# A planner's schedule replaced by a written-out sequence, with the first filter load split in two

## The chip, the cores and the metric

The kernel runs on one core of one Trainium2 chip. Five engines take part, each with its own instruction queue that runs strictly in order: PE (TensorE, matmuls from SBUF into PSUM), DVE (VectorE), ACT (ScalarE), POOL (GpSimd) and SP (SyncE, which here only issues DMAs). They meet through semaphores. The metric is the device time of one execution in microseconds; the time before is the median of three runs.

## The reference

Two layers, each a long convolution mixer followed by an MLP, on a sequence of 2048 rows and 512 channels in bfloat16:

```python
x = A_q
x = x + _A_ref(_layernorm(x), A_k, A_v, A_shift_k, A_ssm_k, A_ssm_D)
x = x + _B_ref(_layernorm(x), B_w1, B_b1, B_w2, B_b2)
x = x + _A_ref(_layernorm(x), A_k, A_v, A_shift_k, A_ssm_k, A_ssm_D)
x = x + _B_ref(_layernorm(x), B_w1, B_b1, B_w2, B_b2)
```

`_A_ref(q, k, v, ...)` shifts `k` along the sequence with four taps per channel, multiplies it with `v` to give `kv`, convolves `kv` causally over 2048 steps with a filter `ssm_k` per channel (by FFT in the reference), adds `kv * ssm_D` and multiplies by `q`. `_B_ref` is a layernorm, a 512 to 1376 matmul with bias, GELU, and a 1376 to 512 matmul with bias. The convolution doesn't depend on `x`, so both layers use the same result `y`, and it is computed once.

## The kernel before

The convolution is an FFT written as small matmuls. A group is usually 16 matmuls that fill two of the eight PSUM banks (1024 float32 columns), and one instruction of ACT or DVE that evicts it to SBUF as bfloat16. The steps, with their PE and eviction lines:

- **ht**: the filters, loaded as four blocks of 128 channels (L679), are turned by 16 PE transposes each (L749) and evicted; `ssm_D` is added to one row (L755, "D" below).
- **h1** (16 groups, L766) and **h2** (16 groups, L779): the two stages of the filter's transform. Stage 2 multiplies by the 4 MB table `S`, which is loaded in 16 pieces.
- **swaps**: 16 DMAs inside SBUF (L647) that make a copy of the transformed filter with neighbouring partitions exchanged. The first eight need the first eight h2 groups, the others the rest.
- **fir**: the shift and `kv`. Channel blocks 0 and 1 go over PE: a turn of `k` (L810, evicted; "T") and two groups of diagonal matmuls (L827), each multiplied with `v` out of PSUM by DVE (L834; "m0", "m1"). Blocks 2 and 3 are eight DVE tensor-tensor instructions each (helper line L658).
- **x1** (16 groups, L766) and **x2** (two halves of eight groups, L872): the same two stages for `kv`. Each x2 group is evicted and then multiplied with the filter by DVE (L658, 128x2048; "P0" to "P7", and "P'0" to "P'7" for the second half).
- **i1** (two halves of eight groups, L896; the second is written `i1'`) and **i2** (ten groups, L953): the inverse stages, which leave `y` in SBUF. A half's i1 needs all eight products of that half.

All evictions of this part go through one helper (L663 on ACT, L664 on DVE). Then come the MLP layers. Layer 0 goes through the rows in blocks of 1, 1, 2, 2, 2, 2, 2, 2, 2 (times 128 rows), layer 1 in four blocks of 4. For each block: **q** (DVE statistics L985 and L987, a power on POOL L991 and L993, the normalization L1000), **y** (two DVE tensor-tensors per row tile), **z** (statistics and normalization again), a transpose (by PE for the first two row tiles, L1047; by a DMA for all others, L1039), **m1** (44 matmuls L1060, 11 GELUs on ACT L1065), **m2** (11 matmuls per row tile, L1093; the last tile in pieces, L1082) and the residual add on DVE (L1097). Row tiles are 16 per layer.

The order of all this isn't the order of the source. Every operation is recorded with estimated durations, reads and writes. A list planner (`schedule`) then places them, by a priority built from the longest path behind an operation, a bias per step (`BIAS`), a bias per operation (`PB`), times before which an operation is held (`HOLD`) and fixed engines for some evictions (`ENG`). DMAs get a priority that keeps them in the order of the source. The planner also gives out PSUM banks, within limits per pool:

```python
dconv = Pool(2, 4, True)
ptr, pm1, pm2 = Pool(1, 2), Pool(1, 3), Pool(1, 3)
```

`sync` then finds the semaphore waits that the resulting order needs, and `emit` writes the five queues.

Of the kernel before, what the change touches and what calls it, by code (L numbers as in the profile page):

```python
# [7 lines left out]
ALU = mybir.AluOpType  # L8
# [14 lines left out]
class Pool:  # L23


    def __init__(self, nb, cap, gate=False):
        self.nb, self.cap, self.used, self.gate = nb, cap, 0, gate


class Tile:  # L30


    def __init__(self, pool):
        self.pool = pool
        self.base = None
        self.left = 0
        self.ops = []


class Op:  # L40
    __slots__ = ("i", "engs", "eng", "fn", "dur", "preds", "succ", "prio", "tile", "dma", "start", "end",
                 "pos", "inc", "waits", "val", "npred", "ready", "bytes", "base", "extra", "gate", "tag", "allow")


class Prog:
# [5 lines left out]
    LAT = 155.0  # L51
    BIAS = {'': 1044190, 'fir0': 816272, 'fir1': 594035, 'fir2': 1000293455, 'fir3': 475782, 'h1': 868926, 'h2': 42492, 'ht': 880650, 'i1_0': 1240071, 'i1_64':
        1212024, 'i2_0': 1097582, 'i2_64': 1190749, 'm1': 1032413, 'm2': -1808312, 'q0': 602778, 'q1': 1095651, 'q19': 267875, 'q2': 1096365, 'q20':
        912832, 'q21': 583017, 'q22': 318772, 'q3': 998981448, 'q4': 986060, 'q5': 466064, 'q6': 470208, 'q7': 409268, 'q8': 641212, 'taps': 736508,
        'warm0': 1000949769, 'x1_0': 1331587, 'x1_1': 783401, 'x1_2': 1063685, 'x1_3': 949292, 'x2_0': 377017, 'x2_64': 955361, 'y0': 1650539, 'y1':
        1623078, 'y19': 2204116, 'y2': 1000018107, 'y20': 947043, 'y21': 1812233, 'y22': 1073869, 'y3': 1411221, 'y4': 607830, 'y5': 295728, 'y6':
        405240, 'y7': 620020, 'y8': 1895488, 'z0': 999281074, 'z1': 1641796, 'z19': 1050878, 'z2': 131483, 'z20': -312548, 'z21': 457235, 'z22':
        577125, 'z3': -403715, 'z4': 81537, 'z5': 198870, 'z6': -330710, 'z7': 181103, 'z8': 1650154}
    SHY = {'fir0': 1021, 'fir1': 277, 'h1': 55, 'h2': 0, 'ht': 0, 'i1_0': 0, 'i1_64': 365, 'i2_0': 61, 'i2_64': 0, 'x1_0': 0, 'x1_1': 8, 'x1_2': 1351, 'x1_3':
        1268, 'x2_0': 0, 'x2_64': 462, 'z0': 261, 'z1': 833}  # L60
    PB = {0: 150814, 1: -52106, 2: -225577, 3: -123331, 4: 999221868, 9: 1276405, 44: 1379512, 45: 1434690, 47: 506509, 49: 453148, 51: 999588645, 52:
        1000042154, 53: 1589169, 54: 1589469, 55: 1517533, 56: 1595021, 57: 1561543, 58: 1589849, 59: 1505754, 60: 1589135, 61: 1539763, 63:
        999477473, 64: 999472326, 65: 81483, 66: 1000044663, 67: 999459987, 68: 19356, 69: 999454615, 70: 999472376, 71: -54290, 72: 999450473, 73:
        999474703, 75: 999467239, 76: -144374, 77: 999428971, 78: 239791, 79: 999491599, 80: 245756, 81: 999824582, 82: 168731, 83: 999955057, 84:
        -153184, 85: 1000209098, 86: 182551, 87: 999183272, 88: 316431, 89: 999956485, 90: -132325, 91: 999955107, 92: 228777, 93: 999458556, 94:
        -263977, 95: 1000286130, 96: -155038, 97: 999951289, 98: 491335, 99: 999392283, 100: 370445, 101: 999956535, 102: 370055, 103: 999943327, 104:
        316481, 105: 1000160828, 106: 1184366, 107: 1000314641, 108: 1291204, 109: 1000854551, 110: 1266991, 111: 1000849866, 112: 1230810, 113:
        1262509, 114: 1184316, 115: 745385, 116: 899745, 117: 1262559, 118: 909647, 119: 1001022447, 120: 893995, 121: 1000704463, 122: 834188, 123:
        874451, 124: 883372, 125: 1000706919, 126: 774582, 127: 998790820, 128: 785190, 129: 1000706969, 130: 861289, 131: 998997835, 132: 820442,
        133: 998980303, 134: 656521, 135: 998997885, 136: 907870, 137: 998958853, 155: -39187, 156: -120533, 157: -28284, 158: -97856, 159: 55705,  # L70
        161: -516310, 162: -336038, 163: -518892, 164: 205143, 165: 997729962, 166: -214054, 167: -532152, 169: 999878049, 170: 26055, 171: 341414,
        172: 302525, 173: -46374, 175: -516143, 176: -99172, 177: 431557, 178: -1035368, 179: 998060916, 180: -4231, 181: 998061019, 183: -127374,
        184: -999854529, 185: -1000132297, 186: -999488136, 187: -999485498, 188: -999373078, 189: -999483119, 191: 998075025, 192: -336655, 193:
# [119 lines left out]
    def __init__(self, nc):  # L193
        self.nc = nc
        self.ops = []
        self.state = {}
        self.nodes = [(-1, None)]
        self.cache = {}
        self.tag = ""
# [62 lines left out]
    def op(self, eng, fn, dur, reads=(), writes=(), tile=None, dma=None, prio=0.0, nbytes=0, gate=()):  # L262
        o = Op()
# [10 lines left out]
        for t in o.tile:  # L274
            for p in t.ops:
                preds.add((p.i, "psum"))
            t.ops.append(o)
            t.left += 1
# [294 lines left out]
NWARM = 0  # L573
# [560 lines left out]
```

## Time and profile before

| what | value |
|---|---|
| time, median of 3 runs | 241.92 us (241.72 to 242.06) |
| the profiled execution: span from first to last instruction | 239.8 us |
| the profiled execution: other times | none is given |
| PE busy | 226.5 us (94%) |
| DVE busy | 175.7 us (73%) |
| ACT busy | 142.9 us (60%) |
| POOL busy | 34.8 us (15%) |
| granted TensorE clock | 1.00 throughout |
| moved by DMA | 27.40 MB, 385 GB/s in slices 2 to 4 of 40 |

The profile is of one execution. Busy shares are means over a span that has two very different parts: the convolution, up to about 84 us, in which PSUM groups are evicted one by one, and the MLP layers, in which PE streams long matmuls. A share over the whole span therefore says little; the chain of waits, the timelines and the windows are read by stage. Where a helper records many operations they share its line (L658, L663, L664), and the shape tells them apart.

### The profile page before, as it was taken

The numbers are of one execution on the slowest core, as the hardware profiler recorded it, in microseconds if no ns is written. First come the engines' busy times: TensorE is split into PE (matmuls) and PEld (weight loads), VectorE is DVE, ScalarE is ACT, GpSimd is POOL, SyncE is SP. The second block draws the span as 40 slices with busy tenths as digits, with TensorE's granted clock in tenths as the row PEclk, the third lists the DMA queues.
The fourth block names the chain that finished last, engine by engine and source line by source line (L and its number), as shares of the span: only waits on it lengthen the run. The fifth ranks groups of instructions, "written<-read, shape, count | busy, mean of one in ns | idle before, by whom it ended". The sixth has DMA issues, their size and how long they took to land.

```text
span 239.8 us, 5559 instructions
## 1 busy us (share of the span) xinstructions
PE 226.5 (94%) x2310; PEld 151.5 (63%) x2330; DVE 175.7 (73%) x363; ACT 142.9 (60%) x223; POOL 34.8 (15%) x75
## 2 busy tenths in 40 slices
PE   7988899886899999999999999999999999999996
PEld 3876777775899885777767665754444444444453
DVE  0779999999997989989999996978997401211214
ACT  3697999999998994665556253464532552436200
POOL 3250000000012222223141032022130100000000
PEclk9999999999999999999999999999999999999999
DMA  6999999999910004222020203313022203210022
GB/s 231 338 387 385 384 235 272 249 282 337 375 63 0 3 0 48 45 44 48 0 44 5 42 1 68 66 23 68 0 44 44 87 3 69 62 44 0 3 98 77
DMA packets 37035, 27.40 MB, mean 114 GB/s; under 512 B 19506, under 2 KB 29969, under 8 KB 37010
## 3 DMA queue, kind: packets, MB, share of 16 engines
q1 hardware_dynamic: 36446, 26.91, 38.1%
q8 instruction: 18, 0.29, 0.5%
q10 hardware_dynamic: 564, 0.14, 0.4%
q14 instruction: 7, 0.06, 0.1%
HBM read 16.82 MB, written 2.10 MB: 79 GB/s over the span
## 4 chain that ended last, share of the span: by engine, by line
PE 71%; DVE 15%; DMA 4%; ACT 4%; SPq 3%; issue 2%; DVEq 0%
PE ps L1060 32%; PE ps L1093 30%; DVE ar L658 8%; PE ps L896 5%; DMA ar<-in_A_v_dram 4%; ACT ar L663 4%; DVE ar L664 4%; SPq L647 3%; DVE ar L834 2%; PE ps L1082 1%; PE ps L872 1%; DVE sm L985 1%; PE ps L953 1%; DVE ar L1000 0%; PE ps L766 0%
## 5 line engine op out<-in xcount | busy, mean ns | idle before, releaser
L1065 ACT ACTIVATE ar<-ps,sm 128x256 bf16<-128x256 f32 (+5 forms) x143 | 67.8, 522 | 72.8 <-PE ps L1060 70.1
L1060 PE MATMUL ps<-ar 128*128 128x256 bf16 (+5 forms) x568 | 83.7, 296 | 0.2
L1093 PE MATMUL ps<-ar 128*128 128x512 bf16 (+1 forms) x329 | 78.9, 379 | 0.7
L663 ACT ACTIVATE ar<-ps 128x1024 bf16<-128x1024 f32 (+2 forms) x79 | 73.9, 1055 | 8.0 <-PE ps L766 3.2
L1060 PEld LDWEIGHTS ps<-ar 128*128 128x128 bf16 (+1 forms) x572 | 53.2, 100 | 29.4 <-ACT ar L1065 0.4
L658 DVE TENSOR_TENSOR ar<-ar 128x512 bf16<-128x512 bf16 (+3 forms) x108 | 63.8, 628 | 1.8 <-DMA ar<-in_A_k_dram 1.4
L1093 PEld LDWEIGHTS ps<-ar 128*128 128x128 bf16 (+1 forms) x341 | 33.2, 98 | 34.5
L1097 DVE TENSOR_TENSOR ar<-ar,ps 128x512 bf16<-128x512 bf16 x31 | 20.8, 682 | 43.2 <-PE ps L1093 43.1
L985 DVE BATCH_NORM_STATS2 sm<-ar 128x6 f32<-128x512 bf16 (+1 forms) x68 | 42.6, 650 | 0.3
L1000 DVE TENSOR_SCALAR ar<-ar,sm 128x512 bf16<-128x512 bf16 x64 | 24.1, 401 | 6.6 <-POOL sm L993 6.3
L993 POOL TENSOR_TENSOR sm<-sm 128x2 f32<-128x2 f32 (+2 forms) x26 | 20.5, 787 | 2.2
L766 PE MATMUL ps<-ar 128*64 128x128 bf16 x512 | 17.6, 221 | 3.0 <-DVE ar L664 1.0
L991 POOL TENSOR_SCALAR sm<-sm 128x2 f32<-128x2 f32 (+2 forms) x26 | 5.9, 226 | 95.9 <-DVE sm L987 95.7
L766 PEld LDWEIGHTS ps<-ar 128*64 128x64 bf16 x512 | 14.9, 110 | 5.4 <-DVE ar L664 1.3
L664 DVE CAST ar<-ps 128x1024 bf16<-128x1024 f32 (+1 forms) x15 | 17.5, 1181 | 0.4 <-PE ps L872 0.2
L896 PE MATMUL ps<-ar 128*128 128x128 bf16 x256 | 15.1, 220 | 1.0 <-DVE ar L658 0.5
L896 PEld LDWEIGHTS ps<-ar 128*128 128x128 bf16 x256 | 14.5, 114 | 1.4 <-ACT ar L663 0.8
L872 PE MATMUL ps<-ar 128*128 128x64 bf16 x256 | 9.6, 193 | 2.3 <-ACT ar L663 2.1
L664 DVE COPY ar<-ps 128x2048 bf16<-128x2048 bf16 (+1 forms) x6 | 5.7, 954 | 7.6 <-PE ps L749 7.4
L987 DVE BATCH_NORM_AGGREGATE sm<-sm 128x2 f32<-128x6 f32 (+1 forms) x64 | 10.8, 177 | 0.6
L872 PEld LDWEIGHTS ps<-ar 128*128 128x128 bf16 x256 | 8.2, 98 | 3.5 <-ACT ar L663 3.4
L779 PE MATMUL ps<-ar 128*128 128x128 bf16 x128 | 8.7, 220 | 0.9 <-ACT ar L663 0.8
(33 smaller groups left out, 72.0 us busy)
## 6 DMA issues: line engine op xcount, KB each, us to landing
ar<-tab_s SPq DMA_DIRECT2D x16, 256.0 KB, 10.0
ar<-ar SPq DMA_DIRECT2D x16, 256.0 KB, 4.6
ar<-in_A_ssm_k_dram SPq DMA_DIRECT2D x4, 512.0 KB, 5.5
ar<-in_A_k_dram SPq DMA_DIRECT2D x8, 256.0 KB, 7.7
ar<-in_A_v_dram SPq DMA_DIRECT2D x8, 256.0 KB, 9.7
ar<-in_A_q_dram SPq DMA_DIRECT2D x4, 512.0 KB, 7.8
out_dram<-ar SPq DMA_DIRECT2D x7, 256.0 KB, 2.0
ar<-in_B_w_dram SPq DMA_DIRECT2D x1, 1376.0 KB, 12.0
```

The lines of the kernel that those rows point to most:

```text
L658: return P.op(eng, lambda e: e.tensor_tensor(o, a, b, op), dur, reads=[a, b] + list(more), writes=[o])
L663: return e.activation(dst, src(), AF.Copy)
L664: return e.tensor_copy(dst, src())
L766: r = e.matmul(Q(tl, 64 * ri, 64, i * 128, [1, 128]), w, m, start=True, stop=True)
L896: r = e.matmul(Q(tl, 0, 128, i * 128, [1, 128]), w, m, start=q == 0, stop=q == 1)
L985: P.op(DVE, lambda e, sj=sj, x=x: e.bn_stats(sj, x), 40.0 + 1.1 * w, reads=[x], writes=[sj], gate=gate)
L993: P.op(POOL, lambda e: e.tensor_tensor(r, v, hf, ALU.pow), 430.0 + 150.0 * n, reads=[v, hf], writes=[r])
L1000: P.op(DVE, lambda e: e.tensor_scalar(o, x, m, r, ALU.subtract, ALU.mult), 335.0, reads=[x, m, r], writes=[o])
L1060: r = e.matmul(Q(tl, 0, rows, 0, [1, w]), a, m, start=dk == 0, stop=dk == 3)
L1065: P.op(ACT, lambda e, dst=dst, tl=tl, rows=rows, bias=bias, w=w: e.activation(dst, Q(tl, 0, rows, 0, [1, w]), AF.Gelu_apprx_tanh, bias=bia ...
L1093: r = e.matmul(Q(tl, 0, 128, 0, [1, 512]), ins[fc][0], ins[fc][1], start=fc == 0, stop=fc == 10)
L1097: P.op(DVE, lambda e, x=x, tl=tl: e.tensor_tensor(x, x, Q(tl, 0, 128, 0, [1, 512]), ALU.add), 640.0, reads=[x], writes=[x], tile=tl)
```

## The change

The planner and its tables are removed. In their place stands a list `ORDER` with the number of every operation, in one sequence over all engines; each engine's queue is that sequence, filtered. `SECOND` names the 20 operations that take the second of their possible engines, and `BANKS` the first PSUM bank of every tile. The limits per pool, the gates on some statistics and the estimated durations go. `sync` and `emit` stay as they were, but for how an eviction's engine is chosen.

One piece of the computation is cut differently: the filters are loaded, turned and evicted as five blocks, two of 64 channels and three of 128. That makes one DMA, one group, one eviction and one add more (1118 operations for 1114).

```diff
+HBLOCKS = ((0, 64), (64, 64), (128, 128), (256, 128), (384, 128))
...
-    for b in range(4):
-        dma(A(0, 128, R_HRAW + b * 2048, [1, 2048]), dr(A_ssm_k, b * 128 * 2048, [2048, 128], [1, 2048]), 1 << 19)
+    for c, n in HBLOCKS:
+        dma(A(c % 128, n, R_HRAW + c // 128 * 2048, [1, 2048]), dr(A_ssm_k, c * 2048, [2048, n], [1, 2048]))
...
+    for c, n in HBLOCKS:
+        tl = Tile(-(-n // 64))
+        src = [A(c % 128, n, R_HRAW + c // 128 * 2048 + a, [16, 128]) for a in range(16)]
+        idn = A(c % 128, n, R_ID + c % 128, [1, n])
...
+                r = e.transpose(QB(tl, 0, 128, a * n, [1, n]), src[a], idn)
...
+    ORDER = (
+        48, 49, 6, 0, 1, 66, 67, 9, 50, 51, 7, 75, 5, 3, 8, 69, 76, 2, 63, 13, 77, 52, 20, 4, 53, 70, 108, 109, 19, 12, 15, 104, 28, 14, 68,
...
+    SECOND = (
+        64, 67, 70, 71, 73, 74, 76, 81, 87, 93, 107, 171, 173, 183, 211, 217, 222, 291, 297, 328)
...
+    def arrange(self):
+
+        self.order = {e: [] for e in (PE, ACT, DVE, POOL, SP)}
+        last = [None] * 8
+        second = set(self.SECOND)
+        assert sorted(self.ORDER) == list(range(len(self.ops)))
+        for at, i in enumerate(self.ORDER):
+            o = self.ops[i]
+            o.eng = o.engs[i in second]
+            o.at, o.pos = at, len(self.order[o.eng])
+            self.order[o.eng].append(o)
+            tl = o.tile
+            if tl is not None and tl.base is None:
+                tl.base = self.BANKS[tl.i]
```

What the lists make of the queues, from the start to the last product (DVE and ACT) and to the first transposing DMA (SP). "ht0a" and "ht0b" are the half blocks (ht0 is block 0 before), "x1.c.n" is group n of channel block c, "fir2.0" to "fir2.7" are the instructions of a DVE channel, "q1" is a statistics instruction of block 1; on SP "k" are the filter blocks, K, V, S, T, X the pieces of `k`, `v`, the tables and `q`, "sw" the swaps.

```text
DVE before: ht0 D0 ht2 h1.2 D2 D1 ht3 D3 h1.6 h1.12 fir2.0 fir2.1 fir0.T fir3.0 fir2.2 fir3.1 fir0.m0
  fir3.2 fir2.3 fir3.3 fir0.m1 h2.3 fir2.4 h2.5 x1.0.0 fir2.5 fir3.4 fir2.6 fir1.m1 h2.8 fir2.7 fir3.5
  fir1.m0 fir3.6 x1.1.0 fir3.7 x1.2.3 x1.3.2 x2.3 P3 P1 P2 P0 P5 P7 P4 P6 P'3 P'0 P'2 P'7 P'1 P'4 P'6 P'5
DVE after: ht0b ht3 D3 ht1 D0b ht0a D0a h1.14 ht2 h1.7 h1.1 h1.4 fir3.0 fir2.0 fir2.1 fir1.T fir2.2
  fir3.1 fir1.m1 fir2.3 fir3.2 fir2.4 fir0.m1 fir2.5 fir2.6 fir3.3 fir0.m0 fir3.4 fir2.7 fir3.5 fir1.m0
  fir3.6 x1.0.3 fir3.7 x1.1.2 x1.3.0 x2.1 P2 P1 P3 P0 P6 x1.3.3 P7 P5 P4 P'3 q1 P'2 q1 P'1 P'0 P'7 P'6 P'5 P'4
ACT before: table tap tap ht1, 13 h1, fir1.T, 6 h2, 3 x1, 7 h2, 8 x1, x2.1 x2.2 x2.0 x2.5 x1.3.0
  x2.7 x2.4 x2.6 x2'3 x2'1 x2'0 x2'2 x2'7 i1.0 x2'4 i1.7 x2'6 x2'5
ACT after: table tap table tap, 12 h1, fir0.T, 14 h2, 2 x1, 2 h2, 6 x1, x2.2 x2.3 x2.0 x1.3.1 x1.2.1
  x2.6 x1.3.2 x2.7 x1.2.2 x2.5 x2.4 x2'3 x2'1 x2'2 x2'0 x2'7 i1.2 x2'6 x2'5 x2'4
SP before: k0 k1 k2 k3 2 halo, K0 to K7, V0 to V7, S0 to S15, tables, T3 sw0 to sw7, sw8 to sw15,
  T0 T1 T2 X0 X1 X2 X3 W1 W2
SP after: k0b k3 k1 k0a k2 K0 K7 K6 halo K2 V7 K1 K3 K5 K4 halo S0 V5 S3 S6 S13 S7 V6 S4 V4 S5 S12 S2
  V3 S10 S1 S15 S14 U S9 V2 V1 S11 V0 S8 bias sw1 sw0 sw5 sw2 bias sw3 sw11 sw14 sw10 sw6 sw15 sw9
  sw4 sw8 X2 T0 sw7 X1 T3 X0 bias T2 sw13 sw12 W2 W1 T1 X3
```

On POOL the adds D1 and D2 and two fills of borders now stand among the eight tap multiplies (L741 before). Behind the products, statistics of blocks 3, 4 and 5 stand earlier on DVE than before, block 0 comes before block 1 on PE (before it was the other way round), and PE's order of m1 and m2 groups is another, with the same groups in it.

## The prediction

> **What bounds the kernel now.** I read the chain that ended last first, in order of time, then each engine's timeline over the first 90 us, then the work in the stretch behind it. The chain:
>
> ```profile
> 52.62 2.29 ACT ar L663 x3
> 54.91 0.44 issue
> 55.35 0.87 ACT ar L663
> ...
> 64.70 3.84 PE ps L896 x64
> 68.63 8.21 PE ps L896 x144
> 76.83 0.45 PE ps L953 x4
> ```
>
> Columns are start, length, what. Up to 64.7 us the chain hops between VectorE and ScalarE, with PE pieces of half a microsecond between; from 64.70 it stays on PE (the 0.9 us pieces of VectorE at 78 to 83 us belong to block 0 and run while PE does the rest of `i2`). The window behind it:
>
> ```profile
> 84.70:237.50 152.80, 151.92 (x928) 88.26 (x941) 101.52 (x267) 68.66 (x144) 22.37 (x42) 1.00 0.18 39
> ```
>
> PE is busy 151.92 of 152.80 us at full granted clock: the two MLP layers have no hole to win. So the end is the moment at which PE becomes continuous, plus a fixed sum of matmuls. That moment is set by VectorE and ScalarE, which turn PSUM groups over. VectorE, then ScalarE:
>
> ```profile
> 16.80 2.36 DVE L658 TENSOR_TENSOR ar<-ar 128x2048 bf16<-128x2048 bf16 x2 [1.43 <-DMA ar<-in_A_k_dram]
> ...
> 50.23 18.25 DVE L658 TENSOR_TENSOR ar<-ar 128x2048 bf16<-128x2048 bf16 x16
> ```
>
> ```profile
> 18.53 1.94 ACT L663 ACTIVATE ar<-ps 128x1024 bf16<-128x1024 f32 x2 [0.53 <-PE ps L766]
> 21.03 1.94 ACT L663 ACTIVATE ar<-ps 128x1024 bf16<-128x1024 f32 x2 [0.56 <-PE ps L766]
> 23.57 2.88 ACT L663 ACTIVATE ar<-ps 128x1024 bf16<-128x1024 f32 x2 [0.60 <-PE ps L766]
> 26.75 14.78 ACT L663 ACTIVATE ar<-ps 128x1024 bf16<-128x1024 f32 x16 [0.31 <-PE ps L779]
> ```
>
> VectorE waits for `k` until 16.80 and then hardly stops until the last product ends at 50.23 + 18.25 = 68.48; PE starts the second half's `i1` 0.15 later, at 68.63. One 1024-column eviction steps at 14.78/16 = 0.92 us on ScalarE, one large VectorE instruction at 18.25/16 = 1.14.
>
> **Part 1, who evicts.** Between first tap and last product VectorE does 45 large instructions before: 16 of the two VectorE channels, 4 PSUM multiplies, 16 products, 9 evictions (fir0.T, three h2, four x1, one x2). That is 51.68/45 = 1.148 each with its small waits. After, 6 evictions are left (fir1.T, four x1, one x2), 42 instructions, and the statistics and their aggregate for `q1` stand between products: 0.60 + 0.10. The first tap still needs all of `k`, now with one 256 KB piece of `v` ahead in SP's queue: 0.262 MB at the 385 GB/s of slice 3 is 0.68, so 16.80 becomes about 17.5. Then 17.5 + 42 x 1.148 + 0.7 = **66.4** for the last product: 2.1 earlier, if nobody starves VectorE.
>
> ScalarE takes what VectorE gave. Up to the last product's eviction it does 55 evictions and one turn (1.88) before, and 56 and one turn after: 53.4 us. Before it begins at 9.48 and has to be done by 68.48 - 1.14 = 67.34; 9.48 + 55 x 0.92 + 1.88 = 62.0, so between 4 and 5 us of gaps lie in it (the rows above, and 0.70, 0.61, 0.44 and smaller ones). After it begins at about 9.2 (part 2): 62.6 plus gaps. Those at 18 to 24 us come from PE sitting behind `fir0.T` and a bank that VectorE held; after, that turn stands at the end of h1, and h2 finds its tables earlier (part 3). I count half the old gaps, 2.2: 64.8, the last product at about 66.0 by ScalarE against 66.4 by VectorE. The two rarely fit without loss; I take **67.0**, a gain of 1.5. The ends are 66.4 (no loss) and 68.3 (all old gaps, 62.6 + 4.5 + 1.2).
>
> **Part 2, the halves.** Before, the first turn starts at 4.97 (16 matmuls, 1.22 us) and four blocks need 4.9 us of PE. After, two half blocks with a 64-column operand (the 64-column matmuls of L872 go 16 in 0.64) and three whole ones: the same PE time. One eviction, one add and one DMA issue are new: about 0.65 for a half eviction (half of the 1.22 row; bounds 0 and 1.22), 0.22 for an add, 0.42 on SP. The half lands first and block 3 second, so a first h1 group can be evicted near 9.2 instead of 9.48, and ScalarE no longer has the 1.88 us turn of block 1. The turns lie before VectorE's wait for `k`, which covers 1.43 us; VectorE's list there (five turns, four h1, three adds) ends near 16.7, before `k`. If it ended later, each microsecond would go straight onto 17.5. A second table load (1.28, its row) now stands between the two tap evictions; ScalarE idles 1.28 there before, so nothing is late.
>
> Two of the adds and two small fills move onto POOL among the tap multiplies, whose eight take 5.55 us from 10.42 and end at 15.97 before. After, the last two or three run past 17 us, beside VectorE's tensor-tensors. No row of before shows that pair. Bounds: nothing, or 2 x 0.69 if VectorE waits out two; I take nothing and keep 1.4 for the range. The Trainium skill (SBUF — State Buffer, "SBUF: two separate sides") says that a GpSimd instruction reading SBUF and a VectorE one with two SBUF inputs exclude each other for a whole instruction; by it the same 1.4 us would be lost, and VectorE would finish at 67.8.
>
> **Part 3, the transfers.** SP's list is another: `S` tables and `v` pieces alternate, the upper swaps are mixed with `X` and `T` loads. Every swap is still behind the h2 evictions that it reads. By ScalarE's order the tenth h2 eviction (lower swaps may go) ends near 9.2 + 11.5 + 1.9 + 10 x 0.92 = 31.8, the sixteenth, with two x1 between, near 39.2; before, the swaps were issued at 32.79 and 41.56. Eight issues at 0.8 put the swap that product 6 needs at 45.6, plus the 4.6 us of the issue table: 50.2; VectorE gets there at 17.5 + 29 x 1.148 = 50.8. The `v` pieces for the first PSUM multiply are 7.0 MB into the queue; `k` landed at 16.80 when 5.2 MB had moved for 4.4 queued, so add 0.8: 7.8 MB have moved at about 23.4, needed at 24.4. These fit with half a microsecond; they are why I don't count 66.4.
>
> `q1` statistics between products wait for `X0`. Ahead of and with it the queue has 16.6 MB; the slices of before reach that sum at 54 us, plus 2 to land is 56. VectorE is there at 17.5 + 35 x 1.148 = 57.7. A later landing delays every product behind it.
>
> **Part 4, behind the products.** PE order puts one `i1` group more behind the last product matmul (14 for 13, 0.93 each), which is only moved. From the second half's first `i1` group the remaining PE work is 168.4 before and 167.5 after (nine and eight `i1` groups at 0.93, 64 `i2` matmuls at 0.113, m1 at 0.054 per matmul and 128 columns, m2 at 0.2165 per matmul); measured 237.49 - 68.63 = 168.86, so 0.4 is lost before. With that group at 68.2 (0.15 behind VectorE it could be 67.2; six groups of 0.93 behind the last product matmul near 62.6 make 68.2) PE would end at 68.2 + 167.9 = 236.1 against 237.49: 1.4 earlier.
>
> The lifted limits on MLP banks cost nothing either way: PE lost 0.4 there in all. The new order spends its slack here. From the last product to the norms of block 3, VectorE has 26.7 us of work after and 23.7 before (by 0.60, 0.34, 0.32 and 1.13 per row); from that first `i1` group PE has 30.3 to block 3's m1 after and 33.0 before. Slack is 3.6 + 1.2 against 9.3 + 0.15. The transposing DMA takes 2.5 to land, and VectorE idled 2.9 us from 68.5 to 95 before (its waits for POOL and PE). 4.8 - 2.6 - 2.9 = -0.7. The early statistics should remove part of the POOL waits; I charge 0.2.
>
> **Sum.** 1.4 - 0.2 = 1.2 earlier: span 239.8 - 1.2 = 238.6. The page gives no other time of its execution than the span; the median lies 241.92 - 239.8 = 2.1 above it, and I keep that: **240.7**.
>
> **Rivals.** (a) *The lists mesh fully*: last product at 66.4, first `i1'` group at 67.5, nothing lost behind: PE ends 237.49 - 2.1, time 239.8. For it: ScalarE's gaps had causes that the order removes. Against: fits of half a microsecond in part 3. Chance 0.22. (b) *The change doesn't do what it says*: ScalarE has 0.9 us more to do and keeps its 4.5 us of gaps, the last product stays at 68.3; about 241.8. Chance 0.14. (c) *The other side*: PE starves at block 3's m1 (or block 2's), because VectorE comes late with the norms. It decides when VectorE idles more than 2.2 us between 67 and 94; the kernel is slower than before from 2.2 + 1.4 = 3.6. With 5 us of idle (before's 2.9 and a 2 us wait for X loads) PE waits 2.8: 241.9 - 1.4 + 2.8 = 243.3. For it: a negative remainder in part 4. Against: before PE lost 0.4 in all there, and earlier statistics fill VectorE's waits. Chance 0.20. Forecast, 240.1 to 241.4: chance 0.44.
>
> **The numbers.** 0.2% of the time is 0.5 us, about what a measurement of this kernel tells from no change. Faster takes forecast and (a), 0.66; same (b), 0.14; slower (c), 0.20. The range runs from 239.3 (a with another half microsecond) into the lower part of (c), 242.7; two in ten are left out, most of them above. The forecast's own range is 240.1 to 241.4.
>
> **What would show it.** First tap at 17.2 to 17.8; last product ending at 66.4 to 67.5; ScalarE's gaps from 9 to 50 us under 3; first `i1` group of the second half at 67.3 to 68.5; PE busy over 99% behind it, PE's last matmul near 236.3. Wrong if VectorE's products wait for a DMA, if tensor-tensors beside POOL take over 1.3 us, or if m1 of the first four blocks waits for VectorE or the transposing DMA.

## The result, and the profile after

The changed kernel takes **245.62 us** (244.99 to 246.06, four runs) against 241.95 (241.72 to 242.06, four runs) for the one before on the same chip. The ratio is 1.0151, with a 95% interval of 1.0135 to 1.0167: slower by 3.7 us, where 1.2 faster was forecast. The profiled execution spans 244.3 us (before 239.8); it is the slowest of the four (246.06), so the difference of the spans, 4.5, is larger than that of the medians.

The chain that ended last, in order of time (start, length, what), at the two places that matter:

```profile
65.89 1.20 ACT ar L454
67.09 0.05 issue
67.14 9.31 PE ps L676 x160
...
91.38 0.78 PE ps L862 x4
92.16 3.98 DMA ar<-ar
96.14 0.04 issue
96.18 1.82 PE ps L829 x17
```

PE becomes continuous at 67.14 (before 64.70). And behind it there is a new hole: block 2's m1 waits for a transposing DMA that takes 3.98 us to land. Before, the same DMA takes 3.86 (issued at 90.37, landed at 94.23), and PE has m2 matmuls to do until then:

```profile
91.21 3.19 PE L1093 MATMUL ps<-ar 128*128 128x512 bf16 x14
```

From the issue on, PE had 3.90 of other work before; in the new order of m1 and m2 groups it has 2.52 (92.16 to 94.68). The late landing and the shorter cover make the wait together. The windows show that nothing else is lost there (PE busy is the second number after the window's length):

```profile
67.14:87.20 20.06, 20.06 (x292) 18.85 (x293) 19.70 (x48) 19.68 (x24) 4.62 (x12) 1.00 0.32 115
87.20:97.00 9.80, 8.30 (x111) 6.72 (x110) 9.70 (x31) 7.36 (x22) 4.53 (x9) 1.00 0.15 28
97.00:242.00 145.00, 144.99 (x844) 81.97 (x841) 88.31 (x231) 59.86 (x125) 19.62 (x34) 1.00 0.17 39
```

So the end comes 4.5 later: 2.44 from the moment at which PE becomes continuous, 1.50 from that wait, and 0.93 from the one i1 group that was moved behind the last product, less 0.4 of small losses that before has (all from the two profiled executions). The lists of VectorE and ScalarE show the first part. VectorE:

```profile
21.13 3.67 DVE L451 TENSOR_TENSOR ar<-ar 128x2048 bf16<-128x2048 bf16 x3
26.33 1.23 DVE L454 COPY ar<-ps 128x2048 bf16<-128x2048 bf16 x1 [1.54 <-PE ps L591]
...
65.52 6.87 DVE L451 TENSOR_TENSOR ar<-ar 128x2048 bf16<-128x2048 bf16 x6
```

Its first tap starts at 21.13 (before 16.80, forecast 17.5) and waits for no DMA: VectorE comes late from its h1 evictions. `k` itself is late too. Its last piece landed at 18.38 (before 16.78) and the halo, which the second tap needs, at 19.13, so that an early VectorE would have met 18.4 and not 17.5. It waits 1.54 for fir1.T's turn, and the last product ends at 72.39 (before 68.48). ScalarE:

```profile
13.40 2.85 ACT L454 ACTIVATE ar<-ps 128x1024 bf16<-128x1024 f32 x3 [4.18 <-PE ps L547]
16.65 7.44 ACT L454 ACTIVATE ar<-ps 128x1024 bf16<-128x1024 f32 x8 [0.40 <-PE ps L547]
25.33 57.64 ACT L454 ACTIVATE ar<-ps 128x1024 bf16<-128x1024 f32 x62 [1.24 <-PE ps L547]
```

The first h1 eviction starts at 13.40 (forecast 9.2). Before:

```profile
9.48 1.94 ACT L663 ACTIVATE ar<-ps 128x1024 bf16<-128x1024 f32 x2 [0.16 <-PE ps L766]
```

Behind its start, ScalarE idles only 0.40 and 1.24, less than was allowed for. TensorE says why it starts so late:

```profile
1.31 2.74 PE L500 MATMUL ps<-ar 128*128 128x512 bf16 x6 [1.31 <-POOL ar L494]
4.55 1.17 PE L530 MATMUL ps<-ar 64*128 64x64 bf16 x16 [0.50 <-DMA ar<-in_A_ssm_k_dram]
5.66 1.03 PE L512 MATMUL ps<-ar 1*128 1x512 bf16 x2
6.62 1.93 PE L530 MATMUL ps<-ar 128*128 128x128 bf16 x16
9.28 3.08 PE L530 MATMUL ps<-ar 128*128 128x128 bf16 x32 [0.73 <-DMA ar<-in_A_ssm_k_dram]
12.29 2.61 PE L547 MATMUL ps<-ar 128*64 128x128 bf16 x64
```

Three things: the first h1 group (12.29) stands behind the turns of block 1 and of the other half (9.28, 32 matmuls), for which the queue waits 0.73; a half turn takes 1.17 for 16 matmuls, not 0.6; and a whole turn takes 1.93 (6.62) where before has 1.22:

```profile
4.97 2.44 PE L749 MATMUL ps<-ar 128*128 128x128 bf16 x32
```

The taps, 0.60 before, take 1.03. The page shows a granted clock of 1.00 for these slices, but it shows 1.00 also where the trace has no record of the clock. The first record, 1.00, is at 13.65 us here and at 4.23 before, and up to 13.65 the matmuls step at about half the rate of later ones.

### The profile page after: what moved, and what is told of

Its sections match the earlier page's. It is cut to its first block, busy times and chain, and to the rows that moved or that the text cites. A ratio compares the mean times of both kernels' runs of the same rounds, so it can differ in the third digit from the quotient of the medians.

```text
span 244.3 us, 5618 instructions
## 1 busy us (share of the span) xinstructions
PE 230.8 (94%) x2346; PEld 154.3 (63%) x2346; DVE 171.9 (70%) x359; ACT 142.6 (58%) x228; POOL 40.0 (16%) x77
## 4 chain that ended last, share of the span: by engine, by line
PE 78%; ACT 9%; DMA 5%; DVE 4%; issue 2%; SPq 0%; DVEq 0%; ACTq 0%
PE ps L829 31%; PE ps L862 30%; ACT ar L454 9%; PE ps L676 5%; DMA ar<-in_A_ssm_k_dram 3%; PE ps L547 3%; PE ps L733 3%; DVE ar L451 2%; PE ps L530 2%; DMA ar<-ar 2%; PE ps L653 2%; PE ps L851 1%; DVE ar L615 1%; DVE ar L454 1%; PE ps L591 1%
## 5 line engine op out<-in xcount | busy, mean ns | idle before, releaser
L834 ACT ACTIVATE ar<-ps,sm 128x256 bf16<-128x256 f32 (+4 forms) x143 | 65.4, 525 | 78.8 <-PE ps L829 78.7
L829 PE MATMUL ps<-ar 128*128 128x256 bf16 (+5 forms) x572 | 85.2, 297 | 1.5 <-DMA ar<-ar 1.5
L862 PE MATMUL ps<-ar 128*128 128x512 bf16 (+1 forms) x341 | 82.2, 379 | 0.0
L454 ACT ACTIVATE ar<-ps 128x1024 bf16<-128x1024 f32 (+2 forms) x83 | 75.4, 1041 | 9.2 <-PE ps L547 5.8
L451 DVE TENSOR_TENSOR ar<-ar 128x512 bf16<-128x512 bf16 (+4 forms) x107 | 64.4, 632 | 0.5
L762 POOL TENSOR_SCALAR sm<-sm 128x2 f32<-128x2 f32 (+2 forms) x26 | 7.1, 275 | 125.3 <-DVE sm L758 124.7
L764 POOL TENSOR_TENSOR sm<-sm 128x2 f32<-128x2 f32 (+2 forms) x26 | 21.8, 837 | 2.1
L547 PE MATMUL ps<-ar 128*64 128x128 bf16 x512 | 18.4, 225 | 3.3 <-issue 1.8
L547 PEld LDWEIGHTS ps<-ar 128*64 128x64 bf16 x512 | 15.6, 113 | 5.6 <-issue 2.1
L454 DVE CAST ar<-ps 128x1024 bf16<-128x1024 f32 (+1 forms) x12 | 14.0, 1180 | 2.0 <-PE ps L547 1.8
## 6 DMA issues: line engine op xcount, KB each, us to landing
ar<-in_B_w_dram SPq DMA_DIRECT2D x1, 1376.0 KB, 12.9
```

What stands on the lines that cost most here:

```text
L451: return P.op(eng, lambda e: e.tensor_tensor(o, a, b, op), reads=[a, b] + list(more), writes=[o])
L454: f = {ACT: lambda e: e.activation(dst, src(), AF.Copy), DVE: lambda e: e.tensor_copy(dst, src())}
L547: r = e.matmul(Q(tl, 64 * ri, 64, i * 128, [1, 128]), w, m, start=True, stop=True)
L764: P.op(POOL, lambda e: e.tensor_tensor(r, v, hf, ALU.pow), reads=[v, hf], writes=[r])
L829: r = e.matmul(Q(tl, 0, rows, 0, [1, w]), a, m, start=dk == 0, stop=dk == 3)
L834: P.op(ACT, lambda e, dst=dst, tl=tl, rows=rows, bias=bias, w=w: e.activation(dst, Q(tl, 0, rows, 0, [1, w]), AF.Gelu_apprx_tanh, bias=bia ...
```

## The experiments

"The changed sequence" is that of the changed kernel. Where the block is whole again, its load, turn and eviction stand at the place of the first half. Times are medians; the kernel before had 241.8 to 242.0 in each comparison.

### First: the front, or the sequence behind it

**whole_block0** undoes the split alone:

```diff
-HBLOCKS = ((0, 64), (64, 64), (128, 128), (256, 128), (384, 128))
+HBLOCKS = ((0, 128), (128, 128), (256, 128), (384, 128))
```

> The changed sequence, but the first 128 channels are loaded, turned and evacuated as one whole block at the place of the first half. Theory 1 (the late first h1 eviction, 13.40 us for 9.48, is handed on one to one to the products and the end; it is late because TensorE turns block 1 and the second half before the h1 group that needs neither): one turn of 16 transpositions, 1.5 us at the rate it has there, leaves the queue ahead of that group, so the first h1 eviction starts at 11.6 to 12.0 and the time is 244.0 (243.6 to 244.4). Theory 2 (the new sequence behind the front costs the time, the front is only waiting on it): within 0.3 of 245.6.

244.01, in two clusters: four runs at 241.6 to 241.9, six at 243.9 to 244.7. The profile is of the upper one: first h1 eviction at 12.43, and yet PE continuous at 67.26, no earlier than with the split, as ScalarE idles 2.68 later (1.64 with it). Its turns run at 114 ns a matmul (3.64 for 32). The wait at block 2's m1 is gone.

**h1_before_turns**

```diff
 TensorE: warm ht0b taps ht3
-  ht1 ht0a h1.15 h1.13
+  h1.15 h1.13 ht1 ht0a
```

> The changed sequence with one edit: on TensorE the two h1 groups of block 3 (h1.15 and h1.13) stand ahead of the turns of block 1 and of the first half instead of behind them; loads, halves and all else as in the changed kernel. Theory 1 (order on TensorE makes the first h1 eviction late, and the delay is handed on one to one): block 3 is ready at 10.06, so the first h1 eviction starts at 10.7 to 11.2 for 13.40, the last product ends 2.2 to 2.7 earlier than 72.39, and the time is 243.1 (242.8 to 243.5). Theory 2 (the sequence behind the front is what costs): less than half of it, 244.5 or more.

247.37, ratio 1.0232 (1.0189 to 1.0274): slower than the changed kernel. The first eviction came early, as expected; the delay only moved:

```profile
11.05 1.94 ACT L454 ACTIVATE ar<-ps 128x1024 bf16<-128x1024 f32 x2 [2.09 <-PE ps L547]
15.80 1.02 ACT L454 ACTIVATE ar<-ps 128x1024 bf16<-128x1024 f32 x1 [2.82 <-PE ps L547]
18.11 7.44 ACT L454 ACTIVATE ar<-ps 128x1024 bf16<-128x1024 f32 x8 [1.29 <-PE ps L547]
25.98 57.63 ACT L454 ACTIVATE ar<-ps 128x1024 bf16<-128x1024 f32 x62 [0.43 <-PE ps L547]
```

TensorE waited 1.66 for block 3's add and then worked at half rate up to 13.76, where the clock's first record stands. The order on TensorE is not by itself the cause: what stands behind the two groups is as late as what stood ahead of them was.

**front_of_before**: whole blocks, and up to the end of h1 the order, engines and banks of before.

```diff
-ScalarE: tap table tap, 12 h1, fir0.T ...
+ScalarE: table tap tap ht1, 13 h1, fir0.T ...
-TensorE: warm ht0b taps ht3 ht1 ht0a h1.15 ...
+TensorE: warm taps ht0 ht1 ht2 h1 h1 h1 ht3 h1 ...
```

> The kernel before up to the end of h1 (whole blocks, its loads of the filter, its turns and its 16 h1 groups in its order, engines and banks), the changed kernel's sequence for everything behind it. Theory 1 (all of the loss comes from the front): first h1 eviction near 9.5, last product at 67 to 68.5, time 241.3 (240.6 to 242.0). Theory 2 (the sequence behind the front costs at least half of it): 243.6 or more.

243.61, at the border that was set for theory 2. ScalarE started at 9.5, VectorE's taps at 17.61, and then, in the profiled execution (243.94, the slowest of four), VectorE stood still:

```profile
17.61 3.50 DVE L451 TENSOR_TENSOR ar<-ar 128x2048 bf16<-128x2048 bf16 x3 [2.26 <-DMA ar<-in_A_k_dram]
25.70 1.23 DVE L454 COPY ar<-ps 128x2048 bf16<-128x2048 bf16 x1 [4.59 <-PE ps L591]
```

The changed sequence puts fir1.T's eviction fourth among VectorE's taps, and its turn behind all 16 h1 groups on TensorE. Part of the 4.59 belongs to this execution alone: the granted clock is 0.50 there from 21.86 to 25.27, and the two turns of `k` take 3.35 us together for the 1.96 that they take in taps_ahead_of_fir1T. The other three runs list a clock of 1.00 and take 243.4 to 243.7, so the median doesn't hang on it. The start alone is worth nothing if h1 as a whole isn't earlier. Theory 1, as it stood, has fallen.

**fetch_shifted** asks about the 1.50 at block 2; three matmuls of each product group are done twice, with the same result:

```diff
-                for i, w, m in ins:
+                for i, w, m in ins[:3] + ins:
```

> The changed kernel with three matmuls of each product group done twice (the second write is the same as the first): 48 more matmuls with their weight loads on TensorE, at a place where it waits anyway, so that everything behind them stands 96 instructions later in TensorE's stream. Theory 3 (the wait of 1.5 us at 94.7 comes from a 16 KB transfer of the instruction queue, one for about 128 matmuls, at 94.04, that lies with the transposing DMA issued at 92.16 and makes it land after 4.0 instead of 2.5): the transfer comes near 90 us, that DMA lands in 2.5, the wait is under 0.4 and the time is 244.2 (243.9 to 244.6). Rival (the first transposing DMAs or VectorE's norms are late whatever the fetches do): the wait stays, 245.6 to 245.9.

The wait fell to 0.31, and the time is 245.29 all the same; in the profile PE lost 0.59 and 0.45 elsewhere. The place of the instruction transfer against the DMA goes with the landing in every profile of this table (issue of the second transposing DMA, start of the 16 KB transfer on the instruction queue, landing):

| kernel | issued | transfer | landing takes | PE waits |
|---|---|---|---|---|
| before | 90.37 | 91.53 | 3.9 | no |
| changed | 92.16 | 94.04 | 3.98 | 1.50 |
| after_warm (below) | 91.32 | 93.19 | 4.0 | 1.53 |
| h1_before_turns | 92.81 | 94.72 | 4.0 | 1.51 |
| fetch_shifted | 92.75 | 90.75 | 2.4 | 0.31 |
| whole_block0 | 92.28 | 95.52 | 2.5 | no |
| warm_front (below) | 90.06 | 93.23 | 2.5 | no |

In the four rows where a transfer starts 1.2 to 1.9 after the issue, the DMA lands 1.4 to 1.5 late. The other twelve traces, and the first transposing DMA of each, agree: 3.0 to 4.1 to land with a transfer 0.6 to 1.9 behind the issue, 2.7 to 3.3 with one that had begun up to 0.5 before it, 2.4 to 2.6 with all others. In whole_block0 the DMA lands at 94.74 and PE goes on at 94.79, so the new order has no time to spare there even with a landing of 2.5. The half block's turn puts 32 more instructions (16 matmuls, 16 weight loads) on TensorE and so brings the transfer to that place.

### Second: who is late behind the front, and what the split costs

**split_in_before**: the kernel before, with the split alone.

```diff
 SP, TensorE, VectorE
-  k0 | ht0 | ht0 D0
+  k0a k0b | ht0a ht0b | ht0a ht0b D0a D0b
```

> The kernel before with one part of the change alone: the first 128 filter channels are loaded, turned and evacuated as two blocks of 64, one right behind the other at the place of the whole block. Theory 4 (the loads of 64 partitions slow the transfers: in the three profiles that have them packets of 4096 bytes take 200 to 450 ns between 7 and 10 us, in the three that have the whole block never over 159, and about 0.45 MB less has moved by 12 us): k lands about 1.2 us later, VectorE's first tap starts near 18.0 for 16.80, the time is 242.9 (242.4 to 243.4). Rival (the slow packets lie where nothing waits for them): first tap within 0.4 of 16.8, time within 0.4 of the kernel before.

243.48, ratio 1.0065 (1.0050 to 1.0080): 1.5 slower. 159 packets of 4096 bytes, those of the filter, took over 170 ns by 12 us (22 before). But the first tap doesn't wait for `k`; h1 is late (first h1 group on PE at 10.90 for 8.80). So the price lies in the forecast range and the way of it was wrong.

**taps_ahead_of_fir1T** and **fir0T_to_vector**, both on front_of_before:

```diff
 VectorE: fir3.0 fir2.0 fir2.1
-  fir1.T fir2.2 fir3.1 fir1.m1 fir2.3
+  fir2.2 fir3.1 fir2.3 fir1.T fir1.m1
```

```diff
-ScalarE: 13 h1 evictions, fir0.T, 14 h2
+ScalarE: 13 h1 evictions, 14 h2
-VectorE: fir3.1 fir2.3 fir1.T
+VectorE: fir3.1 fir0.T fir2.3 fir1.T
```

> The combination with the front of the kernel before and the changed sequence behind it, 243.61, where VectorE stood 4.59 us (21.1 to 25.7) at the eviction of fir1.T. One edit: three of VectorE's own taps, which wait for nothing then, stand ahead of that eviction instead of behind it. The eviction itself can't be later by it, so TensorE and ScalarE see no difference there. Theory 5 (VectorE's list is the bound: the 4.59 us are what ate the earlier start): that wait falls to 1.2, last product 3 us earlier, time 240.5 (240.1 to 241.2). Theory 6 (ScalarE's list is the bound: 19.94 busy of 20.00 between 40 and 60 us, and it starts as late as before): VectorE only waits later, time within 0.5 of 243.6.

> The same, and also the eviction of fir0.T (1.88 us on ScalarE) is done by VectorE, between its taps. Theory 6 (ScalarE's list is the bound): ScalarE has 1.88 less to do ahead of its h2 evictions, the last product and the end come 1.5 to 1.9 earlier than in the combination, 241.9 (241.6 to 242.3). Theory 5 (VectorE's list is the bound): 1.2 slower than the run with three taps ahead alone.

242.82 and 244.50. With three taps ahead the wait of 4.59 fell to 1.11, but 2.01 and 0.90 came back at the next two products out of PSUM: only 0.8 was won, nearer to theory 6. Moving fir0.T to VectorE made it worse, which neither theory had: fir1.T's eviction came later there, TensorE's fir1 group waited 2.03 for it, and the h2 groups behind that group came 1.3 later to ScalarE.

**warm_front**: whole_block0 with two more warm-up matmuls.

```diff
-            for i in range(6):
+            for i in range(8):
```

> The kernel with the whole block at the place of the first half (whole_block0), and 8 matmuls of 512 columns in the warm-up for 6, so that TensorE has no gap between the warm-up and the first turn (0.88 us there). Theory 7 (after that gap TensorE runs its matmuls at about half rate up to 14 us, 114 ns each for 76 in turns, though the granted clock says 1.00, and this is what makes the first h1 eviction late): turns at 76 ns, first h1 eviction at 10.0 to 10.8 for 12.43, and if it is passed on 242.0 (241.6 to 242.6). Rival (the rate has another cause, such as the halves or the loads): turns stay at 105 to 115 ns, first eviction at 12 to 12.8, time within its own spread of 241.6 to 244.7.

**242.11**, all ten runs within 241.81 to 242.45, ratio to before 1.0005 (0.9996 to 1.0014). The two clusters are gone. The clock's first record, 1.00, stands at 5.91 (12.29 in whole_block0); the two whole turns behind it go at 69 ns a matmul, and the first eviction starts at 10.63:

```profile
10.63 2.85 ACT L454 ACTIVATE ar<-ps 128x1024 bf16<-128x1024 f32 x3 [0.96 <-PE ps L547]
13.97 2.85 ACT L454 ACTIVATE ar<-ps 128x1024 bf16<-128x1024 f32 x3 [0.48 <-PE ps L547]
17.43 7.38 ACT L454 ACTIVATE ar<-ps 128x1024 bf16<-128x1024 f32 x7 [0.61 <-PE ps L547]
25.12 1.94 ACT L454 ACTIVATE ar<-ps 128x1024 bf16<-128x1024 f32 x2 [0.32 <-PE ps L560]
27.91 52.95 ACT L454 ACTIVATE ar<-ps 128x1024 bf16<-128x1024 f32 x58 [0.85 <-PE ps L560]
```

### Third: the same warm-up elsewhere, and the instruction stream

**after_warm** (the changed kernel, 8 for 6), **split_warm** (split_in_before, 8 for 6), **front_taps_warm** (taps_ahead_of_fir1T, 7 for 6):

> The changed kernel with 8 matmuls of 512 columns in the warm-up for 6, nothing else. Theory 7 (a gap of 0.36 us or more behind the warm-up leaves TensorE at about half rate until 10 to 14 us; seven profiles so far sort that way, and with the whole block the same edit took 244.01 to 242.11): the half turn takes 0.6 to 0.8 for 1.17, the taps 0.6 for 1.03, the first h1 eviction starts at 12.0 to 12.6 for 13.40 (k1 still lands at 9.2), and the time is 243.9 (243.2 to 244.5). Rival (with the halves the rate has another cause, the late block 1): within 0.4 of 245.6.

> The kernel before with the split alone (243.48, where the four turns ran at 83 ns a matmul on average and the first h1 eviction came at 11.59), and 8 matmuls in the warm-up for 6. Theory 7 (most of the split's price is the cold TensorE, as its smaller loads shift the gap behind the warm-up): first h1 eviction near 10.5, time 242.3 (242.0 to 242.6). Theory 4 (its price is the slower transfers): turns warm, but the time stays at 243.2 to 243.6.

> The combination of the front of the kernel before with the changed sequence behind it and three taps ahead of fir1.T (242.82, its turns at 100 ns in the profile), with 7 matmuls in the warm-up for 6. Theory 7: turns at 76 ns, first h1 eviction of ScalarE 0.8 to 1.2 earlier, time 241.5 (241.0 to 242.0), faster than the kernel before at the lower end. Rival (ScalarE's 12 h1 evictions and its two turns bind anyway): within 0.4 of 242.8.

245.56, 243.52 and 243.03: none gained. In two of them the longer warm-up didn't bring the rate, and the clock's first record is at 10.02 (front_taps_warm) and 10.34 (split_warm): front_taps_warm has no gap from 1.56 on and still turned at 104 ns a matmul. The gap, as theory 7 named it, isn't the condition. In both the two matmuls of the taps, with one row each, stand between warm-up and turns; the rate rose 3.5 to 4.5 us behind them. In after_warm the rate did rise, inside the warm-up:

```profile
1.31 3.37 PE L500 MATMUL ps<-ar 128*128 128x512 bf16 x8 [1.31 <-POOL ar L494]
4.61 1.18 PE L530 MATMUL ps<-ar 64*128 64x64 bf16 x16
5.72 0.60 PE L512 MATMUL ps<-ar 1*128 1x512 bf16 x2
6.25 1.22 PE L530 MATMUL ps<-ar 128*128 128x128 bf16 x16
8.94 2.40 PE L530 MATMUL ps<-ar 128*128 128x128 bf16 x32 [1.46 <-DMA ar<-in_A_ssm_k_dram]
11.27 3.52 PE L547 MATMUL ps<-ar 128*64 128x128 bf16 x64
```

Taps 0.60, a whole turn 1.22; and **the half turn still takes 1.18**: 74 ns a matmul for 64 columns, 76 for 128. Then TensorE waits 1.46 for block 1, and the first h1 groups run at half rate again (3.52 for 64 matmuls, 2.26 in warm_front). The window shows the granted clock, third number from the end, at 0.50:

```profile
11.20:14.50 3.30, 3.30 (x64) 3.24 (x65) 1.08 (x4) 2.13 (x3) 2.56 (x6) 0.50 1.06 366
```

All four runs list a mean clock under 1.00 (0.985 to 0.993), so this isn't the profiled one's alone. The sum of ScalarE's start and idle improves by 0.9 in the profile and PE's start with it (66.28), but 1.53 is lost at block 2 as before. The medians are the same (245.62 and 245.56): the two profiled executions, 246.06 and 245.23, stand on opposite sides of them, so the 0.9 isn't shown to be the edit's.

**fir1T_turn_ahead**

```diff
 TensorE (warm_front): fir0.T
-  h1.11 fir1.T
+  fir1.T h1.11
 ScalarE
-  h1.11 fir0.T
+  fir0.T h1.11
```

> warm_front (whole block, 8 warm-ups, 242.11) with two places exchanged: on TensorE the turn of fir1.T stands ahead of the last h1 group instead of behind it, and on ScalarE the eviction of fir0.T ahead of that group's. Theory 8 (TensorE stops at fixed places of its instruction stream: at the 449th and 705th instruction in every profile, 1.0 to 1.8 us at the 705th, when the next 16 KB of instructions have not come; at the 705th stood this turn, for which VectorE waited 1.62 and through VectorE the h2 groups 0.85): the stop stays at the 705th instruction but falls on the last h1 group, VectorE's wait for fir1.T goes to under 0.5, time 241.3 (241.0 to 241.7). Rival (the stop belongs to the turn's own wait for k or a bank): the turn stops where it stands, 242.0 to 242.4.

242.53. The stop stayed at the 705th instruction and fell on the other work, as theory 8 says:

```profile
23.00 0.64 PE L547 MATMUL ps<-ar 128*64 128x128 bf16 x16 [0.80 <-issue]
```

VectorE's wait for fir1.T is gone. But the last h1 group is late, all h2 groups need it, and ScalarE idles 1.98 and 1.05 where it idled 0.32 and 0.85; VectorE waits 3.44 at fir1's product. This profile is of the slowest of ten runs (244.09): its clock fell to 0.50 from 24.73 to 28.14, and the h2 group there took 1.89 for 1.07. Eight of the ten list a clock of 1.00 and take 242.1 to 242.6. So the exchange gained nothing, where 0.8 was expected; how much of the idle time is its price, and not the clock's, this profile doesn't show. In the changed kernel the same stop cuts an h1 group, and in whole_block0 fir1.T's turn:

```profile
24.69 0.61 PE L547 MATMUL ps<-ar 128*64 128x128 bf16 x15 [1.62 <-issue]
```

```profile
25.46 0.95 PE L591 MATMUL ps<-ar 128*128 128x128 bf16 x14 [1.60 <-issue]
```

### Fourth: the parts of the split, and which list binds

**loads_split_only** and **turns_split_only**: the kernel before, with one list for the loads and one for the turns; the first has the loads split, the second, with the two lists exchanged, the turns.

```diff
-HBLOCKS = ((0, 64), (64, 64), (128, 128), (256, 128), (384, 128))
+LBLOCKS = ((0, 64), (64, 64), (128, 128), (256, 128), (384, 128))
+HBLOCKS = ((0, 128), (128, 128), (256, 128), (384, 128))
...
-    for c, n in HBLOCKS:
+    for c, n in LBLOCKS:
         dma(A(c % 128, n, R_HRAW
```

> The kernel before, with the first 128 filter channels loaded as two transfers of 64 but turned and evacuated as one block. The whole split cost 1.5 us there (243.48). Theory 4 (slow transfers are the price): packets of 4096 bytes over 170 ns appear by the hundred as with the split (22 before), less than 3.15 MB has moved by 12 us (3.21 before), time 243.2 (242.8 to 243.6). Theory 9 (the price is the second turn: in after_warm, at full rate, the half turn took 1.18 us and a whole one 1.22, so a half costs as much as a whole): slow packets or not, the time is 242.2 (241.8 to 242.5).

> The kernel before, with the first 128 filter channels loaded as one transfer but turned, evacuated and added to as two blocks of 64. Theory 9 (the second turn is the price): first h1 group 1.2 later on TensorE (10.0 for 8.80), first h1 eviction at 10.6, 32 more instructions ahead of the stop at the 705th, time 243.2 (242.8 to 243.6). Theory 4 (slow transfers): no slow packets, and 242.2 (241.8 to 242.5).

242.31, ratio 1.0021 (1.0003 to 1.0038), with 133 slow packets and 3.06 MB moved in the first 12 us; and 242.95, ratio 1.0041 (1.0023 to 1.0058), with 16 and 3.48 (before 22 and 3.41). The two prices, 0.44 and 1.08, add up to the 1.5 of the whole split: the second turn looks like the larger part, the slower loads like the smaller, though the intervals of the two overlap. Both profiles also have turns at less than full rate (first record of the clock at 9.68; 0.50 from 7.98 to 11.39), so neither is a price of that step alone.

**h2_ahead**, **one_tap_ahead** and **h2_to_vector**, on warm_front:

```diff
 h2_ahead, TensorE
-  h2 h2 fir1.group h2
+  h2 h2 h2 fir1.group
 h2_ahead, VectorE
-  fir3.1 fir1.m1 fir2.3
+  fir3.1 fir2.3 fir1.m1
 one_tap_ahead, VectorE
-  fir2.1 fir1.T fir2.2
+  fir2.1 fir2.2 fir1.T
 h2_to_vector: one_tap_ahead, and one h2 eviction on VectorE, not ScalarE
```

> warm_front (whole block, 8 warm-ups, 242.11) with one h2 group ahead of fir1's first multiply group on TensorE, which waits for VectorE's eviction of fir1.T there, and one tap more ahead of that group's product on VectorE. Theory 6 (ScalarE's list is the bound from 25 us on, each us that it idles before is passed on): its wait of 0.85 at 27.06 goes, dense from 27.1 for 27.91, last product and end 0.8 earlier: 241.3 (240.9 to 241.7), faster than the kernel before. Rival (VectorE, which is as full, binds: it gains nothing by this): 241.9 to 242.4.

> warm_front (242.11) with one more tap of VectorE ahead of its eviction of fir1.T, where it waits 1.62 us. TensorE and ScalarE are not touched. Theory 6 (ScalarE's list is the bound: in the seven kernels with the changed order behind the front, TensorE becomes continuous 52.0 to 52.2 us after the sum of ScalarE's first h1 eviction and its idle time up to 33 us): VectorE only waits later, time within 0.3 of 242.1. Theory 5 (VectorE's list, which shows no gap from 24 to 71 us either, is the bound): 1.1 earlier, 241.0.

> The same, and one h2 eviction (0.92 on ScalarE, 1.14 on VectorE, near 32 us) is moved from ScalarE to VectorE, into the room that the tap left. Theory 6 (ScalarE's list): TensorE continuous 0.9 earlier, 241.3 (240.9 to 241.6), faster than the kernel before. Theory 5 (VectorE's list): as warm_front, 242.1, and 1.1 above one_tap_ahead. If both lists bind together, each hands its wait to the other and both runs stay within 0.4 of 242.1.

243.11, 242.14 and 243.67. In h2_ahead ScalarE's wait of 0.85 went and one of 1.30 came three evictions later. That makes it level with warm_front in the profile, which is of its fastest run (242.53); why the median is 1.0 slower, no trace shows. In one_tap_ahead VectorE's 1.62 fell to 0.46 and 0.88 came back at fir1's product: nothing won, as theory 6 says. In h2_to_vector ScalarE had one eviction less and waits of 0.71 and 1.17 more, because TensorE's next h2 group stood behind a group that VectorE hadn't multiplied yet; no theory had the 1.5 that it lost. No kernel of these runs beats the one before: warm_front and one_tap_ahead are level with it.

What holds through all of them is ScalarE's sum. In the eight kernels that have the changed kernel's list on ScalarE (two neighbours exchanged in fir1T_turn_ahead) and its product groups:

| kernel | first h1 eviction | ScalarE idle up to 33 us | sum | PE continuous | less the sum |
|---|---|---|---|---|---|
| changed | 13.40 | 1.64 | 15.04 | 67.14 | 52.10 |
| whole_block0 | 12.43 | 2.68 | 15.11 | 67.26 | 52.15 |
| h1_before_turns | 11.05 | 4.54 | 15.59 | 67.78 | 52.19 |
| after_warm | 12.37 | 1.80 | 14.17 | 66.28 | 52.11 |
| warm_front | 10.63 | 2.26 | 12.89 | 65.03 | 52.14 |
| fir1T_turn_ahead | 10.27 | 4.36 | 14.63 | 66.66 | 52.03 |
| h2_ahead | 10.19 | 2.75 | 12.94 | 65.11 | 52.17 |
| one_tap_ahead | 10.29 | 2.51 | 12.80 | 64.80 | 52.00 |

And span less PE's continuous start less the wait at block 2 is 175.6 in each. In these eight profiles, whatever ScalarE loses before 33 us, in its start or behind it, ends up in the span one to one. VectorE's list is nearly as dense: first tap plus idle time, taken off PE's continuous start, leaves 43.8 to 44.4. That one_tap_ahead gained nothing speaks for ScalarE; that h2_to_vector lost says that the two lists hang together.

## Why the prediction was wrong, point by point

- **"With that group at 68.2 ... PE would end at 68.2 + 167.9 = 236.1"** failed by its start, not by its remainder. PE had 173.4 us of work from 67.14 to 242.0; from the same point the forecast's terms give six groups of 0.93 and 167.5, 173.1.
- **"After it begins at about 9.2"**, ScalarE's first h1 eviction, is the step that failed: 13.40. The allowance for gaps (2.2) was generous, 1.64. By the table, as an estimate, 9.2 + 2.2 = 11.4 would have made PE continuous at 63.5 and the span 239.1, close to the forecast 238.6; the sum behind that step was right. It failed for three reasons. I didn't read that ht1 and ht0a stand ahead of h1.15 on TensorE, so that block 1's landing (9.23) counts and not block 3's. The term **"the 64-column matmuls of L872 go 16 in 0.64"** was taken from L872, whose stationary operand has 128 rows and which isn't a transpose: a half turn takes 1.18, so "the same PE time" is 1.1 us more and 32 instructions more. And the turns were charged at before's 1.22, where one ran at 1.93, as TensorE's clock was granted in full only from 13.65 on.
- **"16.80 becomes about 17.5"**, and VectorE's list there **"ends near 16.7"**: the text says that each microsecond by which that list is late goes straight onto 17.5. It ended at 21.1, and `k` landed at 18.38, 1.6 later than before and not 0.7. The price of that was named and its chance not seen, as the list was timed with h1 early.
- **"42 x 1.148 + 0.7"**: from 21.13 to 72.39 are 51.26, against 48.9, with waits of 1.54 (fir1.T) and 0.42 (`X0`). Right in kind, 2.4 short.
- **The second table load** costs nothing, as forecast. **"plus 2 to land is 56"**: `X0` was issued at 55.18 only, behind the swaps, and landed at 63.67. VectorE waited 0.42 for it, and not more only because it was late itself.
- **POOL beside tensor-tensors** ("nothing", bounds to 1.4): VectorE's three at 21.13 took 1.22 each for 1.16, while POOL's two multiplies there took 2.96 together, against 0.65 each elsewhere. The Trainium skill ("SBUF — State Buffer", "SBUF: two separate sides") says that the two exclude each other for a whole instruction; the trace agrees, and here POOL waited and VectorE hardly.
- **"I charge 0.2" for the norms of blocks 2 and 3**: 1.50, and not through VectorE's lateness (rival (c) has the place and the wrong cause). The part on the slack was right that the new order spends it: 2.52 us of work behind the DMA's issue for 3.90. "The transposing DMA takes 2.5 to land" was wrong already before, where the one for block 2 took 3.86; here it took 3.98.
- **Rival (c)**, 243.3, had the sign. The range ended at 242.7, since no case had both lists late: the front was held to be covered by VectorE's wait for `k`, and a late h1 was no rival.

What the change costs, then, by the runs: with whole block and a warm TensorE the sequence is level with before (242.11), so the forecast 1.2 of gain isn't there; ScalarE's sum is 12.9 and not 11.4. The first eviction comes at 10.63 and not at 9.2; its idle time, 2.26, is the 2.2 that was allowed, most of it behind the stops in the instruction stream. With the split and the shorter warm-up 3.5 come on top: 2.1 in ScalarE's sum, 1.5 at block 2, both in the profiles. after_warm, which differs from warm_front in the split alone, has the same 3.5 by its median. The 2.1 aren't divided cleanly between late loads, the longer turns and the lower rate, since each run that changed one of them also shifted another.

## What to carry to other kernels

When a list of evictions has no holes, add the start of its first instruction to its idle time up to there: in these runs that sum, and not the start alone, reached the end, and an edit that removes one wait is only worth something if none comes back two instructions later. Before a stage is timed from its data's landing, read what stands ahead of it in its engine's queue, and price a small matmul from one of the same kind: a transpose of half the columns cost as much as the whole. And where runs of one kernel fall into two clusters, look at the step of the first matmuls, as the page's clock reads 1.00 also where nothing was recorded: two more in the warm-up took a scatter of 2.5 us away here.

## What the runs showed of the hardware

- **TensorE's rate.** Whole turns took 1.22 or 1.93 us per 16. The step of the matmuls changes where the trace's records of the granted clock do. The first record, 1.00, stands 2.7 to 3.0 us after the first matmul in before and after_warm (4.23, 4.32), 4.6 in warm_front (5.91), and only at 10.02 in front_taps_warm, with no gap but with the one-row taps in between; ahead of it there is none, and the page shows 1.00. Where a fall was recorded, the page's rows show 0.50: in after_warm from 11.14 to 14.56, 2.2 us behind a wait of 1.46, in fir1T_turn_ahead from 24.73, around waits of 0.46, 0.80 and 1.12 (an h2 group 1.89 for 1.07), in front_of_before from 21.86 behind one of 1.67. These falls last 3.41 us, and the time from a record to the next is a multiple of that. The Trainium skill ("TensorE: Matmul & The Clock Gate", "Part 1: The HAM clock gate") says that the array runs at half rate until it has been busy through one window of about 3.4 us, and that these windows run free of the kernel's start. The 3.41 agrees, and the scatter and the two clusters of whole_block0 fit the second (no run of the lower cluster was profiled). It has the rate fall after an idle window; here the waits named above, less than a window, were enough. The same page ("Part 4: PE-mode transpose") says that transposes don't count as busy; in front_taps_warm the rate rose at 10.02, within 4.98 us of nothing but turns (the 48 matmuls of h1 behind them took 1.53), so here they did. That the taps count as idle would fit, but no run takes them away, and it stays open.
- **The instruction stream.** The page lists the transfers that bring instructions:

```profile
q8 instruction: 18, 0.29, 0.5%
```

  18 transfers of 16 KB for TensorE's 4692 instructions. Between 10 and 30 us, wherever a matmul stood for over 0.45 us and the program gives no releaser, it was at TensorE's 449th or 705th instruction (once at the 704th; counted from 0, with the sequencer's), 256 apart, whatever stood there; such stops took 0.5 to 1.8 us. While the loads run the next transfer starts 3.8 to 5.1 us after such a stop ends, takes 1.0 to 1.1, and TensorE goes on 1.2 to 1.5 after it, as an estimate at least 6.2 us (3.8 + 1.1 + 1.3) for 256 instructions. The 16 h1 groups are 512 instructions and would take 8 to 9 at full rate (48 matmuls in 1.53). In warm_front the profile names a ScalarE eviction as the releaser of such a stop (1.76, at the 705th); its place in the stream tells what it is.
- **Loads of 64 partitions.** With them 133 to 251 packets of 4096 bytes took over 170 ns by 12 us, without them 11 to 50. Why wasn't found.
